# Third subtiles of at most 64 tokens by fp32 matmuls in two halves of the array, and a first product with 128 columns

## The chip, the cores and the metric

The kernel runs on one core of a Trainium2 chip. The metric is the device time of one execution in microseconds (us). The engines are TensorE (PE, with its weight loads shown as PEld), VectorE (DVE), ScalarE (ACT), GpSimd (POOL) and SyncE (SP, which issues most DMAs).

## The reference, cut to what matters

Pooled attention gives 4608 tokens of 512 values. A mixture of experts follows, and then a dense feed-forward layer over all tokens.

```python
skip_score = x @ w_skip
do_compute = skip_score > 0                # the other tokens pass through
xc = x[do_compute]
logits = xc @ w_gate                       # 8 experts
e_idx = np.argmax(logits, axis=1)
...                                        # gate_w: softmax weight of the chosen expert
for e in range(E):
    mask = e_idx == e
    h = np.maximum(xc[mask] @ w1[e], 0.0)  # 512 -> 1024
    y[mask] = gate_w[mask, None] * (h @ w2[e])   # 1024 -> 512
out[do_compute] = xc + y
```

Then `h = x @ w_in; out = (h * sigmoid(h)) @ w_out`, with 2048 hidden values.

## The kernel before

The mixture of experts works in units: up to 384 tokens of one expert, in subtiles s = 0, 1, 2 of 128. How many units there are, whose they are and how many tokens n each has is counted on the chip. One full unit runs ahead of a loop and one behind it; the loop (`tc.For_i`, line 944) runs over the others.

A value that is to be multiplied in fp32r (rounded fp32) is kept as two fp32r numbers, a high and a low part, so that one product is three matmuls: high by high, high by low, low by high. `split` makes such a pair: ACT writes the high part, DVE subtracts it from the source. `conv1(i)` does that to a quarter of an expert's w1 (raw1 to w1h, w1l), `conv2(raw2, f)` to an eighth of its w2 (raw2 to w2h, w2l).

A pass of the loop: SP issues the loads of the w1 of the unit after this one into raw1 (`load_w1`), POOL gathers that unit's token rows into xn (`gather`) and scatters two subtiles of the unit before from y to xa in DRAM. `mm1(n)` is the first product: for each f of 8, 12 matmuls with 128 stationary columns of w1 and n moving columns (tokens), then `split` with ReLU into hh and hl, then `conv2` of the f-th eighth of w2. It has variants for 384, 320 and 256 columns, chosen by n. `second` is the rest: SP loads the next expert's w2 into raw2 (`load2`), PE transposes two of the four chunks of the next tokens (`xtrans((0, 1))`, split into xth and xtl), DVE computes the gates. Then for s = 2 and s = 1, if n > 128 s, `mm2(s)`: 24 matmuls of 512 columns (8 f, three each) into one PSUM bank, which DVE scales by the gate and adds to the token (xr) into y. Behind s = 2 come the scatter of that subtile, DVE's row numbers si for the two other scatters (which wait until the earlier scatter that reads si has landed) and the four `conv1`. At the end `xtrans((2, 3))` and `mm2(0)`.

All engines run in the order that the program is written in (the class `Ordered`); `nc.before` and `nc.after` hold the branches in that order. `tc.If` is a branch that every engine takes by itself from a register; a semaphore counts how far each engine is, and a branch that does less makes up the count.

Of the kernel before, what the change touches and what calls it, by code (L numbers as in the profile page):

```python
# [5 lines left out]
F32 = mybir.dt.float32  # L6
# [6 lines left out]
AF = mybir.ActivationFunctionType  # L13
ALU = mybir.AluOpType
# [4 lines left out]
P = 128  # L19
B, H, S, D = 8, 8, 576, 64  # L20
G = 72
NT = B * S
DM = H * D
# [129 lines left out]
class Kern:  # L153
# [638 lines left out]
    def moe(self, xa, up):  # L792
        nc, tc, c = self.nc, self.tc, self.c
        with tc.tile_pool(name="ms", bufs=1) as s1, \
             tc.tile_pool(name="mw", bufs=2) as s2, \
             tc.tile_pool(name="mp", bufs=2, space=PSUM) as pp:
            raw2, xn, xth, xtl, gi, si = self.raw2, self.xn, self.xth, self.xtl, self.gi, self.si
            hh = s1.tile([P, 8, U * P], F32R, name="hh", tag="hh")
            hl = s1.tile([P, 8, U * P], F32R, name="hl", tag="hl")
            xr = s1.tile([P, U, XW], F32, name="xr", tag="xr")  # L800
            y = self.x4[:, 0:U]

            def keep():
                nc.scalar.copy(xr[:, U - 1], xn[:, U - 1])
                nc.vector.tensor_copy(xr[:, 0:U - 1], xn[:, 0:U - 1])

            def mm1(n, fs=range(8), conv=True):
                for f in fs:
                    ps = self.hp.tile([P, DM], F32, name=f"hp{f}_{n}", tag="hp")
                    i = 0  # L810
                    for w, x in ((self.w1h, xth), (self.w1h, xtl), (self.w1l, xth)):
                        for k in range(4):
                            nc.tensor.matmul(ps[:, 0:n], w[:, k, P * f:P * (f + 1)], x[:, k, 0:n],
                                             start=(i == 0), stop=(i == 11))
                            i += 1
                    self.split(hh[:, f, 0:n], hl[:, f, 0:n], ps[:, 0:n], relu=True)
                    if conv:
                        self.conv2(raw2, f)
                    else:
                        nc.scalar.copy(self.w2h[:, f], raw2[:, f])  # L820

            def scatter(s, other=None, si=si):

                ids = self.s2 if s == 2 and si is self.si else si[:, s:s + 1]
                ins = nc.gpsimd.indirect_dma_start(xa, bass.IndirectOffsetOnAxis(ap=ids, axis=0), y[:, s],
                                                   None, bounds_check=NT - 1, oob_is_err=False)
                if other:
                    tc.declare_no_dep(ins.ins, other.ins, reason="disjoint rows")
                return ins

            def gates():
                L = xr[:, :, DM:XW]
                v = nc.vector
                mx = s2.tile([P, U], F32, name="gmx", tag="gmx")
                v.tensor_reduce(mx, L, AX.X, ALU.max)
                d = s2.tile([P, U, E], F32, name="gd", tag="gd")
                v.tensor_tensor(d, L, bc(mx, 2, E), ALU.subtract)
                nc.scalar.activation(d, d, AF.Exp)
                gt = s2.tile([P, U], F32, name="gt", tag="gt")
                v.tensor_reduce(gt, d, AX.X, ALU.add)  # L840
                v.tensor_scalar(gt, gt, 1e-9, None, ALU.add)
                v.reciprocal(gt, gt)
                return gt

            def mm2(s, gt, between=None):
                ps = (pp if s else self.hp).tile([P, DM], F32, name=f"yp{s}", tag="yp" if s else "hp")
                i = 0
                for f in range(8):
                    if between and f == 4:
                        between()  # L850
                    for h, w in ((hh, self.w2h), (hh, self.w2l), (hl, self.w2h)):
                        nc.tensor.matmul(ps, h[:, f, P * s:P * (s + 1)], w[:, f], start=(i == 0), stop=(i == 23))
                        i += 1
                nc.vector.scalar_tensor_tensor(y[:, s, 0:DM], ps, gt[:, s:s + 1], xr[:, s, 0:DM], ALU.mult, ALU.add)

            load2 = lambda e: self.load_w2(e, raw2)
            for _ in self.slow:
                pass
            while len(self.todo) > 2:
                self.step()  # L860
            self.step()
            mm1(U * P, (0, 1), False)
            self.cpool = pp, "xt", 2, DM
            for f in range(3):
# [7 lines left out]
            for f, n in ((2, 5), (3, 7), (4, 7), (5, 7)):  # L872
                mm1(U * P, (f,), False)
                for _ in range(n):
                    next(units)
            self.read_table(nc.gpsimd)
            mm1(U * P, (6,), False)

            def low2(f):
# [9 lines left out]
            def second(e, cols, nxt, n=None, third=None):  # L889

                if n is not None:
                    load2(e)
                    self.xtrans((0, 1))
                gt = gates()
                self.rows(gi, nxt)
                nc.vector.tensor_scalar(self.s2, cols[:, U - 1:U] if third is None else third, -1.0, None, ALU.add)

                def convert(f):
                    for _ in self.ffn_ops(f):
                        pass  # L900
                    self.ffn_conv3(f)
                    self.ffn_load(f + 3)

                if n is None:
                    self.ffn_abs(0, self.raw1[:, 0], self.raw1[:, 1])
                    convert(0)
                for s in (2, 1):
                    if n is None:
                        mm2(s, gt)
                    else:  # L910
                        with tc.If(n > P * s) as cmp:
                            nc.before(cmp)
                            mm2(s, gt)
                        nc.after(cmp)
                    if s == 2:
                        scatter(s)
                        nc.vector.tensor_scalar(si[:, 0:U - 1], cols[:, 0:U - 1], -1.0, None, ALU.add)
                        if n is not None:
                            self.conv1(0)
                            self.conv1(1)  # L920
                            self.conv1(2)
                            self.conv1(3)
                if n is None:
                    self.xtrans((0, 1))
                    mm2(0, gt, lambda: self.xtrans((2, 3)))
                else:
                    self.xtrans((2, 3))
                    mm2(0, gt)
# [6 lines left out]
            for f in range(4, 8):  # L935
                low2(f)
            next(units)
            second(None, self.table[:, SLOTS:EMPTY], entry(1, 1, EMPTY, dve))
            for s in (1, 0, 2):
                nc.scalar.copy(y[:, s, DM:XW], xr[:, U - 1, DM:XW])  # L940
# [3 lines left out]
            with tc.For_i(0, nu, 1, iteration_sync="reg_based") as u:  # L944
                ld = lambda i, o, hi: nc.value(self.ut[0:1, i, bass.ds(u + o, 1)], hi)
                e = ld(0, 1, E - 1)
                self.load_w1(e)
                keep()
                n = ld(2, 0, U * P)
                cols, third = [self.table[:, bass.ds(ld(i, 0, EMPTY), m)] for i, m in ((1, U - 1), (3, 1))]  # L950
                nxt = ld(1, 2, EMPTY)
                self.gather(gi)
                scatter(1)
                scatter(0)
                with tc.If(n > 320) as cmp:
                    mm1(384)
                with cmp.Else():
                    with tc.If(n > 256) as cmp2:
                        mm1(320)
                    with cmp2.Else():  # L960
                        mm1(256)
                nc.after(cmp)
                second(e, cols, nxt, n, third)

# [22 lines left out]
            gt = gates()  # L987
# [11 lines left out]
            for s in (2, 1):  # L999
# [3 lines left out]
                while done:  # L1003
                    f = done.pop(0)
# [6 lines left out]
            while done:  # L1011
                f = done.pop(0)
# [554 lines left out]
```

## Time and profile before

| | us |
|---|---|
| median of 3 runs | 1315.89 |
| lowest, highest | 1315.4, 1318.23 |
| the profiled execution, its own time | 1316.77 |
| its span, first to last instruction | 1315.0 |

The profile is of one execution, and its instructions are counted in us from the start of the span. Nearly every instruction has line 110, that of the helper that records it, so the groups are told apart by the tiles they write and read: hp is the bank of mm1, yp that of mm2, xtp that of the transposes of tokens, s that of the attention scores. The start of a matmul is measured and its end is modelled, so the pace of a stream is read from starts. "idle before" is the time that an engine stood still ahead of an instruction, and the arrow names what ended it.

### The profile page before, as it was taken

The numbers are of one execution on the slowest core, as the hardware profiler recorded it, in microseconds if no ns is written. First come the engines' busy times: TensorE is split into PE (matmuls) and PEld (weight loads), VectorE is DVE, ScalarE is ACT, GpSimd is POOL, SyncE is SP. The second block draws the span as 40 slices with busy tenths as digits, with TensorE's granted clock in tenths as the row PEclk, the third lists the DMA queues.
The fourth block names the chain that finished last, engine by engine and source line by source line (L and its number), as shares of the span: only waits on it lengthen the run. The fifth ranks groups of instructions, "written<-read, shape, count | busy, mean of one in ns | idle before, by whom it ended". The sixth has DMA issues, their size and how long they took to land.

```text
span 1315.0 us, 20410 instructions
## 1 busy us (share of the span) xinstructions
PE 1263.7 (96%) x6501; PEld 1076.1 (82%) x6502; DVE 853.5 (65%) x1553; ACT 569.4 (43%) x1188; POOL 358.6 (27%) x312
## 2 busy tenths in 40 slices
PE   6899788999989999999999999999999999999998
PEld 5788677988978888878888888788888888888887
DVE  4777776667667677779743325565784657847565
ACT  4666633454445454344433334534353333533321
POOL 4477433222223230322457603101011010111100
PEclk9999999999999999999999999999999999999999
DMA  9988635656556552248845322634356352463532
GB/s 288 294 271 250 211 129 197 202 178 208 181 181 210 196 191 84 89 164 277 280 169 210 141 97 88 224 124 172 120 185 210 142 176 93 163 208 129 176 106 95
DMA packets 94106, 233.77 MB, mean 178 GB/s; under 512 B 15068, under 2 KB 26972, under 8 KB 90375
## 3 DMA queue, kind: packets, MB, share of 16 engines
q1 hardware_dynamic: 86735, 215.82, 49.3%
q0 software_dynamic: 7008, 16.80, 3.9%
q8 instruction: 42, 0.69, 0.2%
q14 instruction: 33, 0.27, 0.1%
q10 hardware_dynamic: 288, 0.20, 0.1%
HBM read 182.58 MB, written 52.89 MB: 179 GB/s over the span
## 4 chain that ended last, share of the span: by engine, by line
PE 57%; DVE 3%; ACT 1%; issue 1%; POOL 0%; DMA 0%; DVEq 0%; ACTq 0%; POOLq 0%
PE yb L110 20%; PE ps L110 17%; PE fh L110 9%; PE fop L110 9%; PE yp L110 1%; DVE fr L110 1%; DVE ft L110 1%; PE hp L110 1%; PE fxp L110 0%; DVE raw L110 0%; PE sx L110 0%; DVE fgl L110 0%; DVE fsg L110 0%; ACT g L110 0%; DMA out<-fo 0%
## 5 line engine op out<-in xcount | busy, mean ns | idle before, releaser
L110 PE MATMUL yb<-wout,g 128*128 128x512 f32 x1152 | 268.5, 391 | 0.8 <-ACT st L110 0.4
L110 PEld LDWEIGHTS yb<-wout,g 128*128 128x128 f32 x1152 | 215.0, 188 | 45.7 <-DMA wout<-wdo 0.8
L110 POOL TENSOR_TENSOR tm<-tm,tm 128x512 f32<-128x512 f32 x24 | 32.1, 1339 | 411.5 <-ACT tm L110 411.5
L110 DVE TENSOR_TENSOR yacc<-yb,yacc 128x512 f32<-128x512 f32 x168 | 116.1, 691 | 38.2 <-PE yb L110 31.1
L110 ACT COPY tm<-ps 128x512 f32<-128x512 f32 x72 | 42.4, 589 | 146.2 <-PE ps L110 144.4
L110 PE MATMUL yp<-w2h,hh 128*128 128x512 f32 x240 | 96.4, 402 | 1.7 <-ACT w2h L110 1.3
L110 PE MATMUL yp<-w2l,hh 128*128 128x512 f32 x240 | 94.3, 393 | 2.2 <-DVE w2l L110 2.2
L110 PE MATMUL yp<-w2h,hl 128*128 128x512 f32 x240 | 94.3, 393 | 0.0
L110 ACT CAST g<-sg 128x512 fp32r<-128x512 f32 x96 | 59.6, 621 | 76.7 <-DVE sg L110 76.7
L110 ACT ACTIVATE hh<-hp 128x256 fp32r<-128x256 f32 (+2 forms) x96 | 41.2, 429 | 118.0 <-PE hp L110 107.0
L110 ACT ACTIVATE prb<-s,mx 128x72 f32<-128x72 f32 x288 | 65.4, 344 | 46.0 <-DVE mx L110 43.7
L110 DVE TENSOR_TENSOR fsg<-fh,fsg 128x512 f32<-128x512 f32 x48 | 33.0, 688 | 80.0 <-ACT fsg L110 80.0
L110 PE MATMUL fh<-w1l,fh 128*128 128x512 f32 x336 | 83.4, 390 | 0.0
L110 DVE TENSOR_TENSOR tm<-ps,tm 128x512 f32<-128x512 f32 x24 | 16.6, 690 | 98.1 <-PE ps L110 98.1
L110 PE MATMUL hp<-xth,w1h 128*128 128x256 f32 (+2 forms) x384 | 71.3, 307 | 5.3 <-issue 2.5
L110 PE MATMUL hp<-xtl,w1h 128*128 128x256 f32 (+2 forms) x384 | 72.2, 306 | 2.3 <-DVE xtl L110 1.9
L110 PEld LDWEIGHTS fh<-w1l,fh 128*128 128x128 f32 x336 | 62.8, 188 | 12.9
L110 DVE SCALAR_TENSOR_TENSOR hl<-hp,hh 128x256 fp32r<-128x256 f32 (+2 forms) x96 | 46.0, 479 | 40.5 <-ACT hh L110 36.6
L110 PE MATMUL hp<-xth,w1l 128*128 128x256 f32 (+2 forms) x384 | 69.9, 304 | 0.0
L110 DVE TENSOR_TENSOR g<-sg,g 128x512 fp32r<-128x512 f32 x96 | 65.7, 686 | 5.5 <-ACT g L110 5.1
L110 DVE TENSOR_TENSOR w2l<-raw,w2h 128x512 fp32r<-128x512 f32 x96 | 65.9, 691 | 3.3
L110 PE MATMUL pv<-vex,pts 120*128 120x148 f32 (+3 forms) x400 | 61.8, 308 | 4.9 <-remote 2.5
(230 smaller groups left out, 2750.2 us busy)
## 6 DMA issues: line engine op xcount, KB each, us to landing
raw<-w SPq DMA_DIRECT2D x88, 512.0 KB, 3.8
wout<-wdo SPq DMA_DIRECT2D x48, 512.0 KB
win<-wdi SPq DMA_DIRECT2D x36, 512.0 KB
w1l<-wdi SPq DMA_DIRECT2D x36, 512.0 KB
xa<-x SPq DMA_DIRECT2D x36, 256.0 KB
fx<-xa SPq DMA_DIRECT2D x9, 1024.0 KB
v<-vR SPq DMA_DIRECT2D x7, 1200.0 KB
fr<-w_in SPq DMA_DIRECT2D x16, 512.0 KB
```

What stands on the lines that cost most here:

```text
L110: ins = f(*a, **k)
```

## The change

Three things are changed. A variant `mm1(128)` is added for units of at most 128 tokens. For a third subtile of at most 64 tokens (256 < n <= 320) the hidden values of that subtile are kept in a new fp32 tile hx instead of in hh and hl, and `mm2_half` makes its second product: 8 fp32 matmuls with 64 stationary columns, for even f into partitions 0 to 63 of the bank and for odd f into 64 to 127, straight from raw2; ACT copies the second half out, DVE adds the first and then combines as before. Since raw2 is now read there, the load of the next w2 is moved from the start of `second` to behind the third subtile's branch.

```diff
+            hx = s1.tile([P, 8, D], F32, name="hx", tag="hx")
...
-                    self.split(hh[:, f, 0:n], hl[:, f, 0:n], ps[:, 0:n], relu=True)
+                    if n == 2 * P + D:
+                        self.split(hh[:, f, 0:2 * P], hl[:, f, 0:2 * P], ps[:, 0:2 * P], relu=True)
+                        nc.scalar.activation(hx[:, f], ps[:, 2 * P:n], AF.Relu)
+                    else:
+                        self.split(hh[:, f, 0:n], hl[:, f, 0:n], ps[:, 0:n], relu=True)
...
+            def mm2_half(gt):
+                ps = pp.tile([P, DM], F32, name="yq", tag="yp")
+                for f in range(8):
+                    o = D * (f % 2)
+                    nc.tensor.matmul(ps[o:o + D], hx[:, f], raw2[:, f], start=(f < 2), stop=(f >= 6),
+                                     skip_group_check=True)
+                o = y[0:D, 2, 0:DM]
+                nc.scalar.copy(o, ps[D:P])
+                nc.vector.tensor_tensor(o, ps[0:D], o, ALU.add)
+                nc.vector.scalar_tensor_tensor(o, o, gt[0:D, 2:3], xr[0:D, 2, 0:DM], ALU.mult, ALU.add)
...
                 if n is not None:
-                    load2(e)
                     self.xtrans((0, 1))
...
                         with tc.If(n > P * s) as cmp:
                             nc.before(cmp)
-                            mm2(s, gt)
+                            if s == 2:
+                                with tc.If(n > 2 * P + D) as cmp2:
+                                    mm2(s, gt)
+                                with cmp2.Else():
+                                    mm2_half(gt)
+                            else:
+                                mm2(s, gt)
                         nc.after(cmp)
+                        if s == 2:
+                            load2(e)
...
-                with tc.If(n > 320) as cmp:
-                    mm1(384)
+                with tc.If(n > 256) as cmp:
+                    with tc.If(n > 320) as cmp2:
+                        mm1(384)
+                    with cmp2.Else():
+                        mm1(320)
                 with cmp.Else():
-                    with tc.If(n > 256) as cmp2:
-                        mm1(320)
+                    with tc.If(n > 128) as cmp2:
+                        mm1(256)
                     with cmp2.Else():
-                        mm1(256)
+                        mm1(128)
```

## Rows read from the trace of the kernel before

**Rows 1.** The page: busy time of each engine, its share and its instructions.
```profile
PE 1263.7 (96%) x6501; PEld 1076.1 (82%) x6502; DVE 853.5 (65%) x1553; ACT 569.4 (43%) x1188; POOL 358.6 (27%) x312
```
**Rows 2.** Groups by form, PE: out<-in, shapes, count, busy us, mean ns, idle.
```profile
L110 PE MATMUL hp<-xth,w1h 128*128 128x256 f32 x160 | 25.9, 283 | 3.1 <-issue 2.5 <-DVEq L944 0.6
...
L110 PE MATMUL hp<-xth,w1h 128*128 128x320 f32 x128 | 24.0, 309 | 0.0
```
**Rows 3.** Timeline of PE, a unit with third subtile: start us, us, operation, count.
```profile
300.26 0.75 PE L110 MATMUL hp<-xth,w1h 128*128 128x320 f32 x4
...
314.69 0.82 PE L110 MATMUL xtp<-ident,xn 128*128 128x128 f32 x6
315.26 0.47 PE L110 MATMUL yp<-w2h,hh 128*128 128x512 f32 x1
...
320.83 0.39 PE L110 MATMUL yp<-w2h,hh 128*128 128x512 f32 x1
...
332.40 0.75 PE L110 MATMUL hp<-xth,w1h 128*128 128x320 f32 x4
```
**Rows 4.** Timeline of PE, attention: scores of a split tile, then of a whole one.
```profile
44.37 1.25 PE L110 MATMUL s<-kbd,q 128*64 128x144 f32 x16
45.55 0.65 PE L110 MATMUL pt<-ident,prb 128*120 128x128 f32 x4
...
120.67 1.15 PE L110 MATMUL s<-kbd,q 128*128 128x144 f32 x8
121.65 0.27 PE L110 MATMUL pt<-ident,prb 128*120 128x128 f32 x1
```
**Rows 5.** Groups by form, weight loads: 128 and 64 stationary columns.
```profile
L110 PEld LDWEIGHTS hp<-xth,w1h 128*128 128x128 f32 x384 | 59.1, 188 | 8.2 <-issue 5.8 <-DVE hl L110 1.3
...
L110 PEld LDWEIGHTS s<-kbd,q 128*64 128x64 f32 x64 | 3.8, 136 | 2.3 <-ACT prb L110 2.2 <-issue 0.2
```
**Rows 6.** Timeline of the weight loads under the split tile's scores.
```profile
44.37 0.98 PEld L110 LDWEIGHTS s<-kbd,q 128*64 128x64 f32 x16 [0.18 <-ACT prb L110]
```
**Rows 7.** Timeline of PE over a branch that is not taken, mm2(2).
```profile
287.31 0.82 PE L110 MATMUL xtp<-ident,xn 128*128 128x128 f32 x6
288.56 0.49 PE L110 MATMUL yp<-w2h,hh 128*128 128x512 f32 x1 [0.43 <-ACT w2h L110]
```
**Rows 8.** Timeline of PE, the unit at 364 and the next mm1.
```profile
364.19 0.64 PE L110 MATMUL hp<-xth,w1h 128*128 128x256 f32 x4
...
375.50 0.82 PE L110 MATMUL xtp<-ident,xn 128*128 128x128 f32 x6
379.40 1.01 PE L110 MATMUL xtp<-ident,xn 128*128 128x128 f32 x6 [3.08 <-DVE xtl L110]
...
389.34 0.82 PE L110 MATMUL hp<-xtl,w1h 128*128 128x256 f32 x2 [1.16 <-DVE xtl L110]
```
**Rows 9.** Timeline of DVE: the unit with third subtile, then the unit at 364.
```profile
327.40 1.02 DVE L110 TENSOR_TENSOR xtl<-xtp,xth 128x384 fp32r<-128x384 f32 x2 [0.17 <-ACT xth L110]
...
383.59 0.17 DVE L110 TENSOR_SCALAR si<-table 128x2 int32 x1 [2.08 <-DMA xa<-x,si]
...
388.63 1.02 DVE L110 TENSOR_TENSOR xtl<-xtp,xth 128x384 fp32r<-128x384 f32 x2 [0.23 <-DVEq L911]
```
**Rows 10.** Timeline of SP: issues of one w2, from the first over us.
```profile
368.93 8.87 SPq L110 DMA_DIRECT2D raw<-w  x4
```
**Rows 11.** DMA issues: count, KB each, median us from issue to landing.
```profile
raw<-w SPq DMA_DIRECT2D x88, 512.0 KB, 3.8
```
**Rows 12.** Groups by form, ACT and DVE: columns as in rows 2.
```profile
L110 ACT COPY tm<-ps 128x512 f32<-128x512 f32 x72 | 42.4, 589 | 146.2 <-PE ps L110 144.4 <-DMA out<-fo 1.8
...
L110 ACT ACTIVATE hh<-hp 128x320 fp32r<-128x320 f32 x32 | 14.0, 438 | 44.9 <-PE hp L110 42.5 <-PE xtp L110 2.4
...
L110 DVE TENSOR_TENSOR yacc<-yb,yacc 128x512 f32<-128x512 f32 x168 | 116.1, 691 | 38.2 <-PE yb L110 31.1
```
**Rows 13.** Timeline of PE, the first pass of the loop.
```profile
218.72 0.39 PE L110 MATMUL hp<-xth,w1h 128*128 128x256 f32 x1 [2.50 <-issue]
```

## The prediction

> **What bounds it now.** I read the page first: TensorE (PE) is busy for 96% of the span [rows 1]. That is a mean over stages, so it says only where to look. Then the matmul groups by form, to see which variants of the loop really ran: one unit is 8 f times 12 products, 32 of them with xth and w1h, so the 160 with 256 columns are five units and the 128 with 320 columns are four [rows 2]. Then PE in order of time through the loop. In a unit with a third subtile nothing stands still: mm1 starts at 300.26, mm2(2) at 315.26, mm2(1) at 320.83, the next mm1 at 332.40 [rows 3]. There PE is the bound, and what PE saves is saved. The unit at 364 us is different: its second transposes and one mm2 are all that follows mm1, so n is 128 or less, and PE waits 3.08 us for xtl ahead of those transposes and 1.16 us in the next mm1 [rows 8]. There DVE is the bound: its si waits 2.08 us for a scatter to land, four conversions of w1 follow, and xtl comes at 388.63 [rows 9].
>
> **Part 1, the third subtile in fp32 halves; four units.** Removed: 24 products of 512 columns, 320.83 - 315.26 = 5.57 us of PE [rows 3]. Added: 8 fp32 products with 64 stationary columns. Attention has both forms. One score call with 128 stationary columns is four fp32 products and shows 8 records, so an fp32 product is two; they start 0.1225 us apart (121.65 - 120.67 over 8), 0.85 ns for each of 144 columns. The split tiles issue 16 records with 64 columns, two products for one half of the array and then two for the other, and need 45.55 - 44.37 = 1.18 us [rows 4]: 9.6 steps, not 16, so the halves run together. 8 x 0.1225 = 0.98, and the 0.20 left is what entering and leaving the halves costs. The change alternates the halves after every product, a finer weave. So 16 records with 512 columns are 8 steps of 512 x 0.85 = 0.436 us, 3.48 us, with the switches 3.68.
>
> Weight loads would be the catch. Under those 16 products 16 loads take 0.98 us together although one takes 136 ns [rows 5, 6]: they lie beside products, and I add nothing. The Trainium skill, page "TensorE: Matmul & The Clock Gate", section "Part 3: Packing small matmuls", speaks against this change: a weight load overlaps a running matmul only if its row group differs, and both halves here use all rows. This trace disagrees for these shapes; the rule's result is the third rival.
>
> Then the join. mm2 is 24 instructions on PE, mm2_half 8, and the rest of the kernel counts PE's steps by a semaphore, so the shorter branch has to make up the count; I assume that PE lets its last product finish for that. A branch not taken shows what it costs: the transposes end at 287.31 + 0.82 = 288.13 and mm2 starts at 288.56 [rows 7], 0.43 us later, where without that the start lies 0.25 ahead of such an end (314.69 + 0.82 against 315.26, [rows 3]). I take 0.6 us. Sum: 3.68 + 0.6 = 4.3, saved 1.27 a unit, **-5.1 us** for four. Bounds: no drain, 4 x 1.9 = -7.5; another at the outer join, 4 x 0.7 = -2.7.
>
> Beside the path: mm1(320) gets one more ACT operation per f, on 64 columns; ACT stands idle 44.9 us over 32 of these f, 1.4 us each, ahead of the operation that it joins [rows 12]. mm2_half ends in an ACT copy from PSUM, a DVE add and the DVE combination that was there: 0.59 and 0.69 us more, by the nearest rows [rows 12]. Queued behind them on DVE are si, the four conversions and xtl(2, 3), which starts at 327.40 [rows 9] and is needed after the xth products of the next mm1, behind 332.40 [rows 3]. Of that slack of 5 us the saving takes 1.3 and the two operations 1.3 at most, so they cost nothing; with the slack gone they would cost up to 1.3 a unit.
>
> **Part 2, mm1 with 128 columns; one unit.** Now 375.50 - 364.19 = 11.31 us for 96 products, 118 ns each [rows 8]. No product of this type with fewer than 256 columns is in the trace. From below: half, 59 ns, -5.6 us. From above: the fp32 pace, 128 columns x 0.85 x 2 = 217 ns, +9.5 us. Nearest are the loads: 188 ns for 128 stationary columns against 136 for 64 [rows 5], so 52 ns per 64 and 104 per 128 in a stream. Each product brings its load, so I take 104 to 113 ns, which saves 0.5 to 1.3 us, and 0.9. What the next unit receives is set elsewhere: by the si that waits for the scatter, and the 4.87 us from there to xtl [rows 9].
>
> **Part 3, w2's load behind the third subtile; all units.** Before, its four DMAs are issued from 368.93 over 8.87 us, inside mm1, each when its part of raw2 is converted [rows 10]. After, SP issues them once PE is past the If, in one burst: about 1 us behind mm1 in units without a third subtile, about 5 us behind it in those with one. Behind them on SP stand only the next w1 loads, which wait for conversions that come later anyway. A DMA of 512 KB lands 3.8 us after its issue [rows 11]; even one behind the other they land after 3.8, 7.6, 11.4 and 15.2. From the burst to the next mm1's first conversion of raw2 are some 12 us, and the last part is needed six f later, 8 us more. Cost there: nothing. What moves is contention. The gathers of xn (during mm1) lose a competitor, so the first scatter behind them starts earlier; the second gains one. For the four other short units I take both as even, 0 (from -1 to +1 us each); in the unit at 364 I let the 0.9 of part 2 and half of the 1.16 stall through: **-1.4** (from 0 to -2.5).
>
> **Part 4, longer loop.** In the first pass PE stands 2.50 us with nothing to wait for, just ahead of a product of the narrow variant [rows 13], where it has jumped over two wide ones. A fourth variant is one more jump: **+0.8** (0 to 2.5), once.
>
> Sum: -5.1 - 1.4 + 0.8 = -5.7 us. The profiled execution took 1316.77, so 1311.1 by its scale; it lay 0.9 above the median of 1315.89, and against that median the forecast is **1310**.
>
> **Rivals.**
> 1. Halves that take turns (the slower side). If two accumulating streams of 512 columns do not run side by side, the 16 records need 16 x 0.436 = 6.98 us, with switch and drain 7.8 against 5.57: 2.2 x 4 = +8.9, in all about +8, 1324. It turns the result once more than some six in ten records run alone. For: rows 4 have 144 columns, and no accumulation. Against: the same rows. Chance 0.08.
> 2. The narrow product at fp32 pace: +9.5, less the 1.16 stall that it fills, -5.1 + 0.8 = +4, 1320. For: nothing narrower than 256 was seen. Against: it stays one record, where fp32 is two. 0.09.
> 3. Loads not hidden in the halves: 8 x 0.136 = 1.1 us a unit, +4.4: 1314.5. Against: rows 6. 0.06.
> 4. The burst delays the second scatter in the five short units by about 0.8 us each, all passed on: -5.7 + 4 = -1.7, 1314. For: the 2.08 us that si waits [rows 9]. Against: the gathers are freed at the same time. 0.14.
> 5. The loop no longer stays loaded, and every pass stalls as the first did: ten stalls of 2.5 us, 1335. The Trainium skill, page "Runtime: NRT & Kernel Launch", section "Instruction fetch mechanics", says that a taken branch beyond the pages held forces a fetch. In the trace one pass of ten stalls although all of them jump: a loop that is held. 0.03.
>
> **How the numbers follow.** Forecast 0.60, its own range 1306 to 1313 (from the bounds of parts 1, 3 and 4, not all at their ends at once). With rivals 3 and 4 it makes 0.80, so the range is **1305 to 1316**. A measurement of this kernel tells about 0.2%, 2.6 us, from no change: 1313.3 and 1318.5 are the borders. Faster: the forecast and a third of rivals 3 and 4, 0.67. Slower: rivals 1, 2 and 5, 0.20. Same: 0.13.
>
> **What would show it.** In the four units with a third subtile: 16 fp32 records in 3.5 us, two starting together, the next mm2 about 4.3 us behind the start of mm2_half, and the next mm1 without a wait for xtl. In the short unit: 96 products 104 to 113 ns apart. On SP: w2's DMAs in one burst, raw2 landed ahead of its conversions. Wrong if the records run singly, if the granted clock falls in or behind the half-array stretch (three times longer than any here), if conversions wait for raw2, or if PE stands idle in later passes.

## The result and the profile after

The changed kernel takes 1331.11 us (median; 1328.3 to 1332.89), 1.011 times the kernel before, with a 95% interval from 1.0097 to 1.0122: slower by some 15 us, where 1310 was forecast. Its profiled execution took 1328.3 us with a span of 1326.5, 11.5 us more than that of before; it was the fastest of its executions, so the trace shows a little less than the median.

PE's busy time hardly differs from [rows 1]:

```profile
PE 1262.6 (95%) x6469; PEld 1068.9 (81%) x6470; DVE 850.9 (64%) x1557; ACT 574.2 (43%) x1224; POOL 354.0 (27%) x312
```

That doesn't mean that no work was saved: the mean granted clock was 0.991, before 0.997, and at the lower clock the same products keep PE busy for longer (where, is told below). What PE waits for between 213 and 560 us, the longest waits first, in the kernel before and then in the changed one (us in total, times, longest):

```profile
PE xtp L110 <- DVE xtl L110: 3.1, 1, 3.1
PE hp L110 <- issue: 2.5, 1, 2.5
PE hp L110 <- PEq L1563: 1.5, 1, 1.5
PE hp L110 <- DVE xtl L110: 1.3, 2, 1.2
```

```profile
PE hp L110 <- DVE xtl L110: 9.6, 3, 4.5
PE hp L110 <- PEq L1589: 4.4, 1, 4.4
PE xtp L110 <- DVE xtl L110: 2.7, 1, 2.7
PE hp L110 <- issue: 2.6, 1, 2.6
PE yp L110 <- ACT xth L110: 1.3, 1, 1.3
```

Two lines have grown: mm1 waits for xtl (1.3 to 9.6 us), and the mm1 behind the loop waits for PE's sequencer (PEq, 1.5 to 4.4; L1563 and L1589 are the line of the tile context around the whole program). This second wait is that for the loop to end.

The parts that should be faster are faster. The unit with a third subtile, on PE (it answers to [rows 3]), and the groups of the new operations (count, then busy us and mean ns, then idle time):

```profile
320.57 0.82 PE L110 MATMUL xtp<-ident,xn 128*128 128x128 f32 x6
321.32 3.65 PE L110 MATMUL yq<-raw,hx 128*64 128x512 f32 x16
324.90 0.50 PE L110 MATMUL yp<-w2h,hh 128*128 128x512 f32 x1
```

```profile
L110 PEld LDWEIGHTS yq<-raw,hx 128*64 128x64 f32 x64 | 4.2, 136 | 7.5 <-issue 7.5
...
L110 ACT ACTIVATE hx<-hp 128x64 f32<-128x64 f32 x32 | 7.1, 223 | 23.9 <-DVE hl L110 19.6 <-DVE w2l L110 3.8 <-issue 0.5
```

From the transposes to mm2(1) it is 324.90 - 320.57 = 4.33 us, where [rows 3] had 320.83 - 314.69 = 6.14: 1.81 us saved a unit, more than the 1.27 of the forecast. The unit of 38 tokens at 366 us (it answers to [rows 8]) and the mm1 behind it:

```profile
366.79 0.56 PE L110 MATMUL hp<-xth,w1h 128*128 128x128 f32 x4
...
377.46 0.84 PE L110 MATMUL xtp<-ident,xn 128*128 128x128 f32 x6
380.99 1.54 PE L110 MATMUL xtp<-ident,xn 128*128 128x128 f32 x6 [2.68 <-DVE xtl L110]
...
394.12 1.02 PE L110 MATMUL hp<-xtl,w1h 128*128 128x256 f32 x2 [4.53 <-DVE xtl L110]
```

mm1 takes 10.67 us instead of 11.31, 111 ns a product. But the wait in the next mm1 is 4.53 us where it was 1.16. Now SP, POOL and DVE there (they answer to [rows 9, 10]); the second scatter of the kernel before, whose si is the 383.59 of [rows 9], was issued here:

```profile
380.67 1.01 POOL L110 DMA_INDIRECT xa<-x,si  x1 [4.36 <-DMA xa<-x,si]
```

In the changed kernel:

```profile
378.53 2.49 SPq L110 DMA_DIRECT2D raw<-w  x4
380.87 1.00 POOL L110 DMA_INDIRECT xa<-x,si  x1 [2.68 <-DMA xa<-x,si]
388.37 0.17 DVE L110 TENSOR_SCALAR si<-table 128x2 int32 x1 [5.30 <-DMA xa<-x,si]
393.41 1.02 DVE L110 TENSOR_TENSOR xtl<-xtp,xth 128x384 fp32r<-128x384 f32 x2 [0.23 <-DVEq L926]
```

Counted from the start of its unit, the second scatter is issued earlier than before, after 380.87 - 366.79 = 14.08 us instead of 380.67 - 364.19 = 16.48, because mm1 is shorter and the first scatter lands sooner (POOL waits 2.68 us for it, before 4.36). But before, si followed the scatter after 383.59 - 380.67 = 2.92 us, and now after 7.50. So si comes 21.58 us into the unit instead of 19.40. Everything behind si keeps its length (5.04 us from si to xtl in both), so xtl is 2.18 us later in the unit; the next mm1 starts 1.19 us sooner, and the two together are the 3.37 us by which its wait grew.

Behind that wait the granted clock falls. The stretch from the first product with xtl on, before and in the changed kernel (columns: us, busy and instructions of PE, PEld, DVE, ACT, POOL, then PEclk, DMA share, GB/s):

```profile
389.30:392.70 3.40, 3.25 (x26) 3.11 (x27) 2.74 (x6) 1.50 (x4) 0.62 (x1) 1.00 0.91 355
```

```profile
394.10:397.50 3.40, 3.27 (x15) 3.12 (x16) 2.59 (x5) 0.89 (x2) 0.65 (x1) 0.57 0.95 372
```

PE starts 15 products there instead of 26.

What the DMA engines moved while the scatter waited is seen by queues (packets, MB, share of 16 engines' time); q1 are SP's loads, q0 is POOL's. First from the end of the scatter's issue to 385.6, then the 2.4 us behind that:

```profile
DMA packets 613, 1.18 MB, mean 319 GB/s; under 512 B 37, under 2 KB 37, under 8 KB 613
...
q1 hardware_dynamic: 613, 1.18, 97.2%
```

```profile
DMA packets 276, 0.63 MB, mean 262 GB/s; under 512 B 35, under 2 KB 35, under 8 KB 276
...
q1 hardware_dynamic: 196, 0.36, 39.2%
q0 software_dynamic: 80, 0.27, 27.2%
```

For 3.7 us not one packet of the scatter goes out, while 613 of the loads do; its 80 follow when 0.36 MB of the loads are left. So a scatter issued behind the burst waits for most of it: 1.7 of 2.1 MB had gone by then. The Trainium skill, page "DMA: Bandwidth & Descriptors", section "Queues, rings and completion order", says that each DMA engine goes round its queues and changes over after every packet. By that one would expect the scatter to be mixed in among the loads well before. This trace does not show that. It doesn't refute the rule, because how many of the profile's packets (1.9 KB each here) make up one of the page's is not shown.

Why a burst: the four loads of one w2 were issued over 8.87 us inside mm1 [rows 10] and leave now within 2.49 us. SP has a new wait (us in total, times, longest):

```profile
SPq L110 <- PE yq L110: 39.1, 10, 9.7
```

PE is now a reader of raw2, so all four parts become free at one moment, when PE passes the third subtile's branch. In a short unit that is 1.1 us behind mm1, just as the gathers are done and the scatters start.

### The profile page after: what moved, and what is told of

Same layout as the page of the kernel before. It is cut to its first block, busy times and chain, and to the rows that moved or that the text cites. A ratio compares the mean times of both kernels' runs of the same rounds, so it can differ in the third digit from the quotient of the medians.

```text
span 1326.5 us, 20493 instructions
## 1 busy us (share of the span) xinstructions
PE 1262.6 (95%) x6469; PEld 1068.9 (81%) x6470; DVE 850.9 (64%) x1557; ACT 574.2 (43%) x1224; POOL 354.0 (27%) x312
## 4 chain that ended last, share of the span: by engine, by line
PE 59%; DVE 1%; ACT 1%; issue 0%; POOL 0%; DMA 0%; ACTq 0%; POOLq 0%; DVEq 0%
PE yb L110 20%; PE ps L110 17%; PE fh L110 10%; PE fop L110 10%; PE yp L110 1%; PE hp L110 1%; PE fxp L110 0%; PE sx L110 0%; ACT g L110 0%; DMA out<-fo 0%; DVE fr L110 0%; DVE hl L110 0%; POOL tm L110 0%; DVE fsg L110 0%; ACT tm L110 0%
## 5 line engine op out<-in xcount | busy, mean ns | idle before, releaser
L110 PE MATMUL yp<-w2h,hh 128*128 128x512 f32 x208 | 83.9, 403 | 2.6 <-ACT xth L110 1.3
L110 ACT ACTIVATE hh<-hp 128x256 fp32r<-128x256 f32 (+2 forms) x96 | 38.5, 401 | 108.5 <-PE hp L110 102.9
L110 PE MATMUL hp<-xtl,w1h 128*128 128x256 f32 (+3 forms) x384 | 73.9, 312 | 10.5 <-DVE xtl L110 10.2
L110 PE MATMUL yp<-w2l,hh 128*128 128x512 f32 x208 | 81.6, 392 | 2.3 <-DVE w2l L110 2.3
L110 PE MATMUL yp<-w2h,hl 128*128 128x512 f32 x208 | 81.5, 392 | 0.0
L110 PE MATMUL hp<-xth,w1h 128*128 128x256 f32 (+3 forms) x384 | 73.1, 313 | 8.2 <-PEq L1589 4.4
L110 PE MATMUL hp<-xth,w1l 128*128 128x256 f32 (+3 forms) x384 | 71.4, 309 | 0.0
L110 PEld LDWEIGHTS hp<-xtl,w1h 128*128 128x128 f32 x384 | 61.1, 194 | 12.3 <-issue 11.1
L110 PEld LDWEIGHTS hp<-xth,w1h 128*128 128x128 f32 x384 | 60.9, 194 | 11.0 <-issue 8.8
```

Source lines behind the costliest of these rows:

```text
L110: ins = f(*a, **k)
```

## The experiments

The comparison left three theories: 1, the burst ahead of the second scatter; 2, ACT's hx, which waits for DVE's hl (19.6 us in the group above) and makes both engines lag; 3, the longer code. Each run has its ratio to the kernel before, with the interval. The ratio is what compares: the kernel before was measured again beside each group of runs, with medians from 1314.7 to 1318.3 us.

**The burst alone.**

```diff
                             mm2(s, gt)
+                            if s == 2:
+                                ps = pp.tile([P, DM], F32, name="yq", tag="yp")
+                                for i in range(4):
+                                    nc.tensor.matmul(ps[0:2, 0:2], raw2[:, 2 * i, 0:2], raw2[:, 2 * i + 1, 0:2],
+                                                     start=(i == 0), stop=(i == 3))
                         nc.after(cmp)
+                        if s == 2:
+                            load2(e)      # and no load2(e) at the start of second
```

> The kernel before, and of the change only the late load: behind mm2(2), in units with a third subtile, PE makes four products of two columns that read raw2 (their result goes nowhere), and load2 stands behind the If of s == 2. So w2's four DMAs leave in one burst behind mm1 in every unit, as in the changed kernel, while mm1, hh, hl and mm2 stay as before. Theory 1 (the burst queues ahead of the second scatter, so si, the conversions of w1 and xtl come late in the short units): nearly the whole loss with none of the gain, 1325 to 1338 us, with the second scatter of a short unit landing 8 to 10 us behind its issue instead of about 3, and PE waiting for xtl in mm1. Theory 2 (the extra ACT operation hx, which stands behind DVE's hl, makes ACT and DVE lag): none of it is here, 1315 to 1319 us. Theory 3 (longer loop code, more jumps): 1315 to 1318 us.

Measured: 1333.7 us, ratio 1.0136 (1.0116 to 1.0156). The burst alone costs at least as much as the whole change (1.0110; the intervals overlap); hx and the new variants aren't in it. (The tiny products are 0.7 us of each unit that has them, 32.48 against 31.79 in the table below.) Theories 2 and 3 are no main cause.

**Half of the burst.** `for i in (2, 3)` in the code above, so that only two of the four loads are held back.

> As burst_alone, but the tiny products read only the last two of w2's four parts: the first two leave inside mm1 as in the kernel before, only the last two in a burst behind it. Theory 1 (what is queued ahead of the second scatter sets its delay): half of the bytes, half of the delay, about 2 us instead of 4 in the short units; the stall that is left in mm1 falls by more than half, because part of a delay is covered: 1319 to 1325 us. If the position behind mm1 or the reads by PE are what costs, whatever the bytes: 1330 us or more.

Measured: 1324.04 us, ratio 1.0046 (1.0030 to 1.0061), a third of the loss. The unit of 38 tokens in burst_alone and in half_burst, POOL's second scatter and si:

```profile
384.28 1.01 POOL L110 DMA_INDIRECT xa<-x,si  x1 [2.64 <-DMA xa<-x,si]
391.52 0.17 DVE L110 TENSOR_SCALAR si<-table 128x2 int32 x1 [4.60 <-DMA xa<-x,si]
```

```profile
384.06 1.00 POOL L110 DMA_INDIRECT xa<-x,si  x1 [2.69 <-DMA xa<-x,si]
388.42 0.17 DVE L110 TENSOR_SCALAR si<-table 128x2 int32 x1 [1.89 <-DMA xa<-x,si]
```

From issue to si: 2.92 us with no burst, 4.36 with half, 7.24 with all of it (8 to 10 were expected). The delay goes with the bytes ahead.

**The narrow variant alone**, in the kernel before.

> The kernel before, and of the change only mm1(128) with its fourth branch; load2 stands where it stood. Theories 1 and 2: one unit gains 0.6 us in mm1 and the code is a little longer, 1314 to 1317 us. Theory 3 (longer loop code): 1318 us or more, with the time lost in the first pass or at jumps.

Measured: 1316.3 us, ratio 1.0009 (0.9994 to 1.0024). No gain can be told; in its trace mm1 of the 38-token unit is 0.64 us shorter than [rows 8], and PE then stands 2.72 us for xtl, so most of the unit's time stays.

**hx first**, in the changed kernel.

```diff
-                        self.split(hh[:, f, 0:2 * P], hl[:, f, 0:2 * P], ps[:, 0:2 * P], relu=True)
                         nc.scalar.activation(hx[:, f], ps[:, 2 * P:n], AF.Relu)
+                        self.split(hh[:, f, 0:2 * P], hl[:, f, 0:2 * P], ps[:, 0:2 * P], relu=True)
```

> The changed kernel, with ACT's hx ahead of hh, so that ACT no longer waits for DVE's hl between its two readings of one accumulator. Theory 1 (burst): the waits of PE for xtl in the short units stay, 1326 to 1331 us; only what the lag of ACT and DVE costs at the loop's exit (up to 5 us) can go. Theory 2 (hx chain): 1316 us or less.

Measured: 1327.7 us, ratio 1.0094 (1.0071 to 1.0117): as theory 1 has it. PE's waits for xtl stay (10.7 us). The wait at the loop's end falls from 4.4 to 2.9, but not because the loop's last work comes earlier: POOL's last scatter starts 28.93 us into the last unit (501.62 - 472.69), 27.61 in the changed kernel (501.33 - 473.72). PE itself comes later there. So no gain by this order is shown; the intervals of 1.0094 and 1.0110 overlap too.

**The load early again** in units that don't read raw2 on PE.

```diff
                     with tc.If(n > 320) as cmp2:
                         mm1(384)
+                        load2(e)          # likewise behind mm1(256) and mm1(128)
...
                                 with cmp2.Else():
                                     mm2_half(gt)
+                                    load2(e)
...
-                        if s == 2:
-                            load2(e)
```

> The changed kernel, with load2 in the branches of mm1: in units without the fp32 halves its DMAs are issued inside mm1 again, each as its part of raw2 is converted, and only units of 257 to 320 tokens load behind mm2_half. Theory 1 (burst ahead of the second scatter of the short units): the loss goes and the gain of the halves (some 7 us) shows, 1308 to 1316 us; what is left is the exit of the loop. Theory 2 (hx chain): 1325 us or more. Theory 3 (code): 1325 us or more.

Measured: 1316.98 us, ratio 1.0012 (0.9996 to 1.0028). The loss goes, just outside the upper end of what was expected, but the gain of the halves doesn't show in the sum: PE still waits 4.6 us at the loop's end.

**The same burst, behind the scatter.**

```diff
                         nc.vector.tensor_scalar(si[:, 0:U - 1], cols[:, 0:U - 1], -1.0, None, ALU.add)
                         if n is not None:
+                            for i in range(4):
+                                nc.vector.memset(raw2[0:1, 2 * i, 0:1], 0.0)
+                            load2(e)      # and not behind the third subtile's branch
                             self.conv1(0)
```

> The changed kernel, the same burst of w2's four DMAs in every unit, but behind the second scatter instead of ahead of it: DVE writes one element into each part of raw2 right behind si (which waits for that scatter to land), and load2 stands behind these writes; nothing else is changed (the written elements are loaded over). Theory 1 in the form that the order decides, not the burst (the scatter's packets wait for what was queued before them): the stalls of mm1 go, the exit's loss stays, 1315 to 1322 us. If the burst costs by its contention wherever it stands, or if raw2 now comes too late for the next mm1: 1328 us or more.

Measured: 1317.24 us, ratio 1.0007 (0.9991 to 1.0023). This is the sharpest of the runs: the loads leave as closely together as in the changed kernel, only behind si. The 38-token unit, POOL and DVE, and then SP:

```profile
377.10 1.01 POOL L110 DMA_INDIRECT xa<-x,si  x1 [2.65 <-DMA xa<-x,si]
380.01 0.17 DVE L110 TENSOR_SCALAR si<-table 128x2 int32 x1 [1.27 <-DMA xa<-x,si]
```

```profile
380.40 2.54 SPq L110 DMA_DIRECT2D raw<-w  x4
```

si follows the scatter after 2.91 us, as before. Not the burst costs, but its place ahead of a small transfer for which a chain is waiting. In this profile the ten units of the loop together take 5.6 us less than before, although the last one takes 1.5 more (35.27 against 33.79). The sum shows nothing of it, because 1.9 us more stand ahead of the loop, 1.8 in the mm1 behind it and 4.1 after that. Ahead of the loop and after that mm1 the code is the same. (In the 4.1, PE waits 2.43 us once for ACT, and the granted clock is 0.72 in the 6 us behind that; no other profile has more than 1.6 there.) What the kernel itself still loses stands at the loop's end.

**The loop's end.** PE's next mm1 (its row names PEq) started 10.6 us behind the start of POOL's last scatter in the changed kernel, hx_first, early_load, both_mended, both_no_narrow, gates_early and gates_no_narrow, and 11.4 to 11.6 us in the three kernels where the load stands behind si (why it is longer there is open). That looks as if no engine leaves the loop before POOL is done with that scatter. (Where PE waits only 1.5 us, before, in narrow_alone, burst_alone and half_burst, it is 11.6 to 12.3 us, so there the scatter isn't what PE waits for.) The changed kernel, that scatter, the copy that stands ahead of it, and mm1:

```profile
497.35 0.22 ACT L110 ACTIVATE gd<-gd 128x24 f32<-128x24 f32 x1 [2.47 <-DVE gd L110]
497.90 0.58 ACT L110 COPY x<-yq 64x512 f32<-64x512 f32 x1 [0.33 <-PE yp L110]
...
501.33 1.30 POOL L110 DMA_INDIRECT xa<-x,sq  x1 [8.93 <-DVE si L110]
...
511.92 1.62 PE L110 MATMUL hp<-xth,w1h 128*128 128x384 f32 x4 [4.44 <-PEq L1589]
```

yq starts at 492.00 and is done at 495.65, but ACT copies it at 497.90, because the gates' exponential stands ahead of it in ACT's order and waits for DVE, which lags behind mm1. Two runs take this apart: hx first and the early load together, then that with the gates' operations inside mm1.

```diff
-            def mm1(n, fs=range(8), conv=True):
+            def mm1(n, fs=range(8), conv=True, also=None):
...
+                    if also and f in (3, 4, 5):
+                        next(also)        # gates() in three steps: DVE, ACT's Exp, DVE
...
-                gt = gates()
+                gt = gt or gates()        # in the loop, gt comes from mm1's steps
...
-                        mm1(384)
+                        mm1(384, also=gate_steps(*t))     # likewise the other variants
```

> The changed kernel with both edits: load2 early but for units of 257 to 320 tokens, and hx ahead of hh. Theory 1 with theory 2 as the cause of what was left in early_load (GpSimd's last scatter of the loop comes late because the gates' operations queue behind xtl, and xtl lags): the exit comes 1.5 to 2 us earlier than in early_load, 1312 to 1315.5 us. If the wait of hx for hl has nothing to do with the exit: as early_load, 1316 to 1318 us.

Measured: 1320.08 us, ratio 1.0011 (0.9996 to 1.0026): nothing gained over early_load, against my expectation. The wait at the loop's end did fall from 4.6 to 3.4 us, but the exit comes no earlier: POOL's last scatter starts 24.83 us into the last unit, 24.73 in early_load. And the first pass took longer, by a stall (below).

> As both_mended, with the gates' operations of DVE and ACT inside mm1 (behind f = 3, 4 and 5) instead of behind the first transposes. If the exit of the loop is set by GpSimd's last scatter plus its 9.6 us drain, and this scatter waits for the gates, the exit comes another 1 to 2 us earlier: 1310 to 1314 us. If not: as both_mended, or slower by the delay of DVE in mm1.

Measured: 1313.63 us, ratio 0.9969 (0.9955 to 0.9982): faster than the kernel before. The last scatter starts 22.14 us into the last unit, 2.69 us earlier than in both_mended, and the next mm1 comes earlier by the same 2.69 (32.73 instead of 35.42 us). This is what shows that the scatter sets the exit. The wait at the loop's end is 1.7 us, and the mm1 behind it takes 23.60 us, as before (25.00 in both_mended).

**The first pass.** The first unit of the loop took 27.7 us before, 31.9 in both_mended. These rows of both_mended and of the same kernel without mm1(128) are PE's first mm2 in it, behind the branch not taken [rows 7]:

```profile
230.27 0.79 PE L110 MATMUL yp<-w2h,hh 128*128 128x512 f32 x1 [2.66 <-PEq L926]
```

```profile
229.36 0.49 PE L110 MATMUL yp<-w2h,hh 128*128 128x512 f32 x1 [0.43 <-ACT w2h L110]
```

> As both_mended, without the variant of mm1 for 128 columns (units of at most 128 tokens take 256 columns again). If the variant gives only what its own unit shows, 0.6 us: both_mended plus 0 to 1 us. If its code costs at the first pass (a fetch behind mm1 of the first unit, 1.2 us of idle PE): both_mended less 0.5 to 1.5 us.

Measured: 1314.86 us, ratio 0.9987 (0.9969 to 1.0006), 0.24% below both_mended, though the two intervals overlap. Its first pass takes 28.65 us.

The stall isn't all of that pass. In the stretch from 213 to 232 us the granted clock was lower in some profiles, with mm1(128) or without it. The kernel before and the changed one (columns as above):

```profile
213.00:232.00 19.00, 15.45 (x113) 14.40 (x113) 11.03 (x20) 8.53 (x19) 4.59 (x4) 1.00 0.92 309
```

```profile
213.00:232.00 19.00, 15.66 (x109) 14.53 (x107) 9.54 (x17) 7.56 (x17) 4.57 (x5) 0.91 0.64 225
```

Of the fourteen profiles, three have a first pass without a stretch at the lower clock: before, burst_behind and all_mended_no_narrow, 27.3 to 27.7 us. Those with one and no stall at a branch (narrow_alone, both_no_narrow, gates_no_narrow, burst_alone and half_burst) take 28.2 to 28.7.

> gates_early without the variant of mm1 for 128 columns. In both_mended and gates_early the first pass of the loop took 31.9 and 32.0 us, with TensorE standing up to 2.7 us at a branch behind mm1; without the variant, in both_no_narrow, 28.7. If that is the code of the variant: gates_early less 2 to 3 us, 1309 to 1313 us, 0.4 to 0.6% below the kernel before. If the stall was chance: as gates_early or 0.6 us above it.

Measured: 1310.64 us, ratio 0.9961 (0.9947 to 0.9975). Less than expected against gates_early (0.08%), but at the low end of the range in us. Its first pass takes 28.67 us, that of gates_early 31.97.

**Everything mended**, with the burst behind the scatter: hx first, gates inside mm1; then without mm1(128).

> burst_behind with the two edits for the exit: hx ahead of hh, and the gates' operations inside mm1. In burst_behind what is lost against the kernel before stands in the last unit of the loop (35.27 us from mm1 to the next mm1, 33.79 before) and in the mm1 behind it (25.41 against 23.59). If the burst's place and the exit together are the whole loss of the changed kernel, the last unit falls to 31 to 32.7 us and the mm1 behind it to 23.6: 1309 to 1312.5 us, 0.3 to 0.6% below the kernel before. If the loads behind the scatter bring a loss of their own once the rest is mended: 1314 us or more.

Measured: 1308.97 us, ratio 0.9958 (0.9942 to 0.9974). The last unit takes 32.98 us and the mm1 behind it 23.58, about as expected.

> all_mended without the variant of mm1 for 128 columns. If that variant's code stalls the first pass only in some layouts (it did not in burst_behind, 27.49 us): all_mended plus 0 to 1 us, for the one unit of 38 tokens. If it costs in every layout: all_mended less 1 to 3 us.

Measured: 1304.8 us, ratio 0.9925 (0.9909 to 0.9940), the fastest kernel of this study: the halves of part 1, with the load behind the scatter, the gates early, and no narrow variant. It is 4.2 us below all_mended, more than the 1 to 3 expected. No run has the gates early without the halves, so how much of the gain over the kernel before is due to the halves alone is not shown. PE's waits in it, from 205 us (compare the two lists at the start):

```profile
PE xtp L110 <- DVE xtl L110: 3.3, 2, 2.5
PE hp L110 <- PEq L1599: 2.6, 1, 2.6
PE hp L110 <- issue: 2.3, 1, 2.3
PE yp L110 <- ACT w2h L110: 1.7, 4, 0.4
```

The table puts the runs together: us from the first product of mm1 to that of the next mm1 (from the timelines of PE), for each unit of the loop by its tokens, and for the mm1 behind the loop up to the transposes that follow its first mm2.

| unit | before | changed | burst_alone | half_burst | early_load | burst_behind | all_mended_no_narrow |
|---|---|---|---|---|---|---|---|
| 237, first pass | 27.69 | 29.82 | 28.16 | 28.73 | 29.36 | 27.49 | 27.34 |
| 379 | 34.68 | 34.67 | 36.86 | 35.26 | 34.68 | 34.67 | 34.68 |
| 197 | 24.25 | 24.28 | 24.33 | 24.32 | 24.25 | 24.26 | 24.25 |
| 266, third subtile | 32.14 | 32.87 | 37.05 | 34.23 | 31.57 | 30.14 | 30.14 |
| 311, third subtile | 31.79 | 30.14 | 32.48 | 32.36 | 30.14 | 30.14 | 30.14 |
| 38 | 23.12 | 21.93 | 22.58 | 22.73 | 22.20 | 21.91 | 22.21 |
| 256 | 25.65 | 30.58 | 30.84 | 26.07 | 25.65 | 25.99 | 24.66 |
| 307, third subtile | 32.49 | 30.15 | 32.48 | 32.55 | 30.72 | 30.14 | 30.14 |
| 256 | 24.25 | 24.27 | 24.33 | 24.35 | 24.25 | 24.25 | 24.25 |
| 297, third subtile, last | 33.79 | 38.20 | 39.17 | 35.65 | 35.33 | 35.27 | 32.94 |
| the mm1 behind the loop | 23.59 | 25.96 | 23.60 | 23.59 | 25.52 | 25.41 | 25.26 |

A unit's late scatter is paid by the next unit: 266 behind 197, 256 behind 38, 297 behind 256. In the changed kernel these three hold the waits of 9.6 us.

## Why the prediction was wrong

**What bounds it.** Right where nothing is in front: the third-subtile units of 311 and 307 tokens fell by 1.65 and 2.34 us. But I read [rows 3] as holding for all four. The unit of 266 begins with what the unit ahead of it owes, and the last one ends with the loop.

**Part 1** was right and too cautious. The 16 records take 3.58 us (3.68 forecast), 0.448 a step against 0.436, and there is no drain at the join: mm2(1) starts right behind yq, where I had put 0.6. (The 0.43 us of [rows 7], on which that rested, are in the row itself a wait for ACT's w2h, not for the branch.) Four units give 7.2 us of PE by that, not 5.1; a whole unit in which nothing waits fell by 1.65 (31.79 to 30.14), 6.6 for four. Rival 1 falls with this. Rival 3 falls too: the 16 loads of 136 ns would be 2.2 us a unit if they were not hidden. The rule of the Trainium skill that I weighed there (page "TensorE: Matmul & The Clock Gate", section "Part 3: Packing small matmuls") doesn't hold for these shapes in this trace.

One reading beside the path was incomplete: "ACT stands idle 44.9 us over 32 of these f, 1.4 us each, ahead of the operation that it joins". ACT's time was free, its order was not: hx waits until DVE's hl is done (26 of 32 times). Both read the same bank. The Trainium skill, page "PSUM — Partial Sum Buffer", section "PSUM bank collisions raise a hardware error", says that two engines must not touch one bank and quadrant at once, reads included; the order that the trace shows is what that asks for. No run shows that it costs anything: with hx first the last scatter came no earlier, in hx_first or in both_mended.

**Part 2** was right in pace (111 ns, forecast 104 to 113) and wrong in worth: narrow_alone shows no gain. Without its code one pair of kernels was faster (0.9925 against 0.9958), a second only as far as the overlapping intervals tell (0.9987 against 1.0011), a third not beyond them (0.9961 against 0.9969).

**Part 3** is the step that failed: "For the four other short units I take both as even, 0 (from -1 to +1 us each)". I saw that the first scatter loses a competitor and that the second gains one, and put the two at even without a price. The right number stood in the same paragraph. I worked out that four loads in a row land after 3.8 to 15.2 us at worst, and asked only whether raw2 comes in time, not how long a scatter issued behind them would wait. The first half was right: the second scatter is issued 2.40 us sooner in the 38-token unit. But si then follows its issue 4.58 us later (7.50 - 2.92). The mechanism was rival 4, with the chance of 0.14, and its size was wrong: mm1 waited for xtl 9.6 us behind three of the five short units (2.16, 4.53 and 2.90), 1.3 before, where the rival had 4 in all. From the other two nothing reached PE. For the unit of 38 tokens itself I had put -1.4; it and the unit behind it took 3.74 us more (-1.19 + 4.93). And the rival had no term for the clock behind such a wait: the unit of 256 tokens behind that of 38 grew by 4.93 us, of which its wait is 3.37 and the lower clock the rest.

**Part 4** was too small. The first pass took 2.13 us more, not 0.8. The 2.50 us that I took for the jump's price [rows 13] hardly grew (2.56); they stand behind 15 products of that mm1 (14 in the changed kernel), so that they are the jump's was a guess from the start. But PE then ran slower (11.02 us for the other 82 products, before 9.65 for 81), because the granted clock was 0.81 in 218 to 222 us and 0.76 in 222 to 226, in part at the lower level, where before it was 1.00 through the whole pass. And PE stood 1.30 us ahead of mm2. The stall ahead was as long before, without a fall of the clock behind it, so a fourth variant is not shown to be the cause. The longer stall at the branch comes and goes with the layout: 2.66 us in both_mended, 1.60 in all_mended, none with the variant in narrow_alone (0.43). That it is code being loaded was only argued. No later pass stalls, so rival 5 falls.

**What I hadn't in the sum at all** is the loop's end. The rows for it were in the trace of before: the last scatter at 491.93, mm1 at 503.49, and 1.54 us for PE. What PE saves in the last unit is lost there unless POOL's last scatter comes earlier too. In the changed kernel that is 2.9 us at the gap, and then the clock: in the 6.7 us behind it the granted clock is 0.59 in the mean, most of it at the lower level (1.2 of 2.4 GHz), where before it was 1.00 (the stretches are the mm1 of 384 columns in both; columns as in the other stretches above).

```profile
503.50:510.20 6.70, 6.70 (x39) 6.66 (x39) 6.04 (x9) 4.64 (x7) 3.12 (x2) 1.00 0.11 42
```

```profile
512.00:518.70 6.70, 6.70 (x24) 6.70 (x25) 6.11 (x8) 2.68 (x4) 3.06 (x2) 0.59 0.12 42
```

24 products instead of 39: the mm1 behind the loop took 2.37 us more. The length of the wait alone doesn't tell whether the clock falls. Behind waits of 2.63, 2.92, 3.35, 4.59 and 4.97 us (all_mended_no_narrow, hx_first, both_mended, early_load, burst_behind) it was 0.54 to 0.77 in the same stretch of 6.7 us; behind 2.67 and 3.28 us (all_mended, both_no_narrow) it was 1.00. What decides is open.

**The sum**, for the profiled executions: 1.37 us ahead of the loop, where no code was changed (the first mm1 of the loop starts between 211.3 and 215.5 us in the fourteen profiles, so two executions can differ by that; here the granted clock was 0.57 from 152 to 156 us, before 1.00); 2.13 in the first pass; 0.73 - 1.65 - 1.19 + 4.93 - 2.34 + 4.41 = 4.89 in the units behind it; 2.37 in the mm1 behind the loop; 0.7 later. With the small ones 11.5. The gains are in these numbers, and so are some 5 us at the lower clock: 1.3 in the first pass, 1.6 behind the wait of 4.53 us, 2.4 behind the loop. The median lies 4 us further off; no trace shows where these stand.

## What to carry to other kernels

When a buffer gets a second reader, ask when its parts become free: loads that were spread out by one reader leave in a burst behind the other, and a small transfer issued into that burst waits for it. Price that wait by the bytes ahead and the landing time, and look for a chain that hangs on it. Then look at the granted clock behind each new wait of PE: here it added some 4 us to two waits. A saving in a loop's last pass is worth little until the engine that ends the loop comes earlier too.

## What was not expected of the hardware

- A scatter of 80 packets issued by POOL stood 3.7 us without one packet going out, while SP's queue moved 613.
- From the start of POOL's last scatter to PE's first product behind the loop it is 10.6 us (501.33 to 511.92) in seven kernels, and when that scatter came 2.69 us earlier, so did the product.
- fp32 products with 64 stationary and 512 moving columns, accumulating in two halves of the array, run side by side: 0.448 us for two records, with their weight loads hidden.
- The granted clock was 0.59 in the 6.7 us behind a wait of PE of 4.44 us, and 1.00 behind one of 1.54; between these lengths it went both ways (0.54 behind 2.63 us, 1.00 behind 3.28).
